# One transformer-like kernel: two v buffers, another pace of the transfers, the last pair's scaling moved into the next stage, and the first pair's scores as products of 64 rows

## The chip, the cores and the metric

The kernel runs on one core of one Trainium2 chip. The metric is the device time of one launch in microseconds (us). Before the change it was 1083.71 us, the median of three runs (1082.7 to 1085.96).

## The reference

Attention over 4 batches of 8 heads (576 tokens, 64 columns a head) that keeps only scores within tau of the row's maximum, then two feed-forward layers over the 2304 tokens:

```
scores = q @ k.T / 8;  thresh = max(scores, row) - tau
scores = where(scores >= thresh, scores, -1e9)
attn = exp(scores - max);  attn = attn / (sum(attn) + 1e-9);  a = attn @ v        # x: 2304 x 512
h = x @ w_in;  g = h * tanh(softplus(h));  x2 = g @ w_out                         # 512 -> 2048 -> 512
y = (silu(x2 @ w_gate) * (x2 @ w_val)) @ w_out2                                   # 512 -> 1536 -> 512
```

## The kernel before, in words

**Pairs.** Attention works through 16 pairs of heads, one after the other, overlapped. The two heads of a pair lie in the upper and the lower 64 partitions of q and k. Each fp32 operand is split into a high part (`qh`, `kh`, rounded to fp32r) and the rest (`ql`, `kl`, L222 to L228); a product of scores is high times high plus the two mixed ones. For pairs 1 to 15 SyncE (SP in the profile) copies these parts into one tile `stk` by 12 transfers a pair (L237), head by head, so that 128 rows hold the high and low parts of one head: then a score tile of 128 queries by 576 keys takes four matmuls (L95: two products, each in columns of 320 and 256). Pair 0 has no such copies: before the change the other head's 64 rows of its query tile are set to zero (L254), the two heads' parts are made one after the other (L261, L263), and a score tile takes six matmuls of 128 rows (L104).

**One score tile** i of 9 (four pairs of tiles, head by turns, and one that holds the last 64 rows of both heads) goes PE scores, DVE row maximum (L112), POOL threshold (L116), ACT exponential (L122), DVE mask and row sum into `pp` (L130), PE transposes (L159, into `tg`), ACT copies into `pt` (L165 to L172), and PE products with v (L182: `av` 0 after the first four score tiles, `av` 1 after all). The row sums' reciprocals go to DRAM and come back spread over the partitions (`r`, `rs`, L200, L205), and POOL multiplies them into the output `acc` in place (L216). Scores have three PSUM buffers, transposes and av two together.

**Order.** Every engine works through its queue in order. The order is written by a list scheduler (`Plan`) from costs, buffers (`SLOTS`: what takes a buffer waits for who gave it back) and a table of ranks (`RANK`, `PERIOD`). Transfers too: one queue, SP's, issues all of them, so a transfer that waits for its buffer holds what is queued behind it. The tile of v had one buffer, and another one for the last pair only (`vslot`).

**The second stage** (`moes`) makes the layers by a scheme of seven products for eight: `ha`, `hb` (L808) and `y` (L934, L936), from pieces `xp` of x and from weights that ACT (L503, L507, L536), DVE (L511, L514, L540) and POOL (L517) convert while the stage runs. It has a plan of its own, so every engine's queue holds all of attention and then all of this stage. Before the change the scaling of the last pair (L205, L216) stands at the end of attention.

Of the kernel before, what the change touches and what calls it, by code (L numbers as in the profile page):

```python
# [16 lines left out]
P = 128  # L17
# [19 lines left out]
def attention(tc, cst, q, k, v, x, beside, parked, S=576):  # L37
# [31 lines left out]

    def mine(nm, h):  # L70
        return slice(64, 640) if nm == "k" and h == 0 else slice(0, 576)

    def vslot(p):
        return "vz" if p == NP - 1 else "vn"

    def load(p, nm):
        src = dict(q=q, k=k, v=v)[nm][p]
        if nm == "v":
            t = pw.tile([P, 10, 64], F32, tag=vslot(p), name=f"vn{p}", bufs=SLOTS["vn"])
        else:  # L80
            t = pn.tile([P, KW], F32, tag="n", name=f"{nm}n{p}", bufs=SLOTS["n"])[:, 0:src.shape[1]]
        nc.sync.dma_start(out=t, in_=src)
        st[p][nm + "n"] = t


    def scores(p, i):
        d = st[p]
        s = ps.tile([P, 1024], F32, tag="s", name=f"s{p}_{i}", bufs=SLOTS["s"])[:, 192:768]
        d["s", i] = s
        c, h = divmod(i, 2)  # L90
        for c0, n in ((0, 320), (320, 256)):
            if p and i < 8:
                q0, k0 = (colB if h else colA) + 128 * c, 576 * h + c0
                for w in (1, 2):
                    nc.tensor.matmul(out=s[:, c0:c0 + n], lhsT=d["stk"][:, 0, q0:q0 + P], rhs=d["stk"][:, w, k0:k0 + n], start=w == 1, stop=w == 2)  # L95
                continue
            for w, (a, b) in enumerate((("h", "h"), ("l", "h"), ("h", "l"))):
                if i < 8:

                    q0, k0 = 576 * h + 128 * c + 64 * h, mine("k", h).start + c0  # L100
                    lhsT, rhs = d["stk"][:, "hl".index(a), q0:q0 + P], d["k" + b][:, k0:k0 + n]
                else:
                    lhsT, rhs = d["qt"][:, "hl".index(a)], d["k" + b][:, 64 + c0:64 + c0 + n]
                nc.tensor.matmul(out=s[:, c0:c0 + n], lhsT=lhsT, rhs=rhs, start=w == 0, stop=w == 2)  # L104
# [97 lines left out]
    def spread(p):  # L202
        t = st[p]["rs"] = pw.tile([P, S], F32, tag="rs", name=f"rs{p}", bufs=SLOTS["rs"])
        for a, c0, n, at in ((0, 0, S, 0), (64, 0, 512, 640), (64, 512, 64, 576)):
            nc.sync.dma_start(out=t[a:a + 64, c0:c0 + n], in_=parked[p][at:at + n].partition_broadcast(64))  # L205

    def xout(p, u):
        for to, c0, c1 in xslices(p, 256 * u, 256 + 64 * u):
            if XOUT[u] == "DVE":
                nc.vector.tensor_copy(out=to, in_=st[p]["av", u][:, c0:c1])  # L210
            else:
                nc.scalar.copy(out=to, in_=st[p]["av", u][:, c0:c1])

# [26 lines left out]
    def tails(p):  # L240
        d = st[p]
        d["qt"] = qt[p % 2]
        for w in range(2):
            for h in range(2):
                a = slice(64 * h, 64 * h + 64)
                t = d["q" + "hl"[w]] if p else d["stk"][:, w, 576 * h:576 * h + 576]
# [3 lines left out]
    def zeros(p):  # L250
        d = st[p]
        d["stk"] = pw.tile([P, 3, 1152], F32R, tag="stk", name=f"stk{p}", bufs=SLOTS["stk"])
        for h in range(2):
            nc.gpsimd.memset(f(d["stk"][64 - 64 * h:128 - 64 * h, 0:2, 576 * h:576 * h + 576]), 0.0)  # L254

    def firstparts(p, what, h):
        d = st[p]
        a, cols = slice(64 * h, 64 * h + 64), slice(576 * h, 576 * h + 576)
        hi, lo = (d["stk"][a, w, cols] for w in range(2))
        if what == "hi":  # L260
            nc.scalar.copy(out=hi, in_=d["qn"][a])  # L261
        else:
            nc.vector.tensor_tensor(out=lo, in0=d["qn"][a], in1=f(hi), op=ALU.subtract)  # L263


    turns = {}
    for tag in "gs":
        line = [(PERIOD * p + r, (p, k, i)) for p in range(NP) for k in "STA" for i, r in enumerate(RANK[k + OWN.get(p, "")]) if (k == "S" or f"{k}{i}" in SIDE) == (tag == "s")]
        turns.update({x: (tag, n) for n, (_, x) in enumerate(sorted(line))})
    plan = Plan(SLOTS, WAIT)  # L270
    for p in range(NP):
# [7 lines left out]
        for nm in "qk":  # L279
            op("DMA", .6, load, nm, key=(nm, "load"), take=["n"])  # L280
            if nm == "q":
                op(*(("Pool", (.72, .74), inputs, "q", "scale", nc.gpsimd) if p else ("DVE", .4, inputs, "q", "scale", nc.vector)), key=("q", "scale"), after=[("q", "load")])
            if nm == "q" and p == 0:
                op("Pool", (2.4, 2.42), zeros, key=("q", "zeros"), take=["stk"])
                for h in range(2):
# [5 lines left out]
        op("Pool", (1.13, 1.15), tails, key=("t",), after=[("q", "stack", 1) if p else ("q", "lo", 1)], take=["qt"], free=["q"] * (p > 0))  # L291
        op("DMA", .6, load, "v", key=("v", "load"), take=[vslot(p)])
        for nm, cost in (("q", 1.2), ("k", 2.4)) * (p > 0):
            for h in range(2):
                op("DMA", cost, stack, nm, h, key=(nm, "stack", h), after=[(nm, "lo"), ("q", "stack", 0)][:2 if (nm, h) != ("q", 0) else 1], take=["stk"] * ((nm, h) == ("q", 0)))
        for i in range(9):
            c, h = divmod(i, 2)
            made = [(y, "stack", z) for y in "qk" for z in ([h] if i < 8 else [0, 1])] if p else [("q", "lo", h if i < 8 else 1), ("k", "lo")]
            op("PE", (.53, .74) if p and i < 8 else (.81, 1.03), scores, i, key=("S", i), after=made + [("t",)] * (i == 8), take=[turns[p, "S", i]], free=["k", "qt", "stk"] if i == 8 else [])
            op("DVE", (.67, .753), rowmax, i, key=("R", i), after=[("S", i)] + [("R", 0)] * (i > 0), take=["sm"] * (i == 0))  # L300
# [7 lines left out]
            if i in (3, 8):  # L308
                u = int(i == 8)
                ready = [("V", y, z) for y in ((0, 1), (2, 3))[u] for z in (0, 3, 6)] + [("V", 4, 0), ("V", 4, 4), ("A", 0)] * u + [("v", "load")]  # L310
                t = 5 * (.432, .538)[u]
                op("PE", (t, t + .22), av, u, 0, 5, key=("A", u), after=ready, take=[turns[p, "A", u]], free=["pt"] + [vslot(p)] * u)
                t = .335 + .07 * u
                op(XOUT[u], (t, t + .09) if XOUT[u] == "DVE" else (.255 + .05 * u, .37 + .05 * u), xout, u, key=("x", u), after=[("A", u)], free=[turns[p, "A", u]])
# [3 lines left out]
        op("DMA", 1.7, park, key=("o", "out"), after=[("Z",)], free=["rr"])  # L318
        op("DMA", 1.3, spread, key=("i", "in"), after=[("o", "out")], take=["rs"])
# [6 lines left out]
    ctx.close()  # L326


class Plan:
# [46 lines left out]
    def order(self, ops, strict):  # L376
# [8 lines left out]
        for o in ops:  # L385
            before = [(made[x], True) for x in o["after"] if x not in self.given]
            for x, k in o["take"]:
                if (x, k - 1) in took:
# [75 lines left out]
GIVEN = dict(DMA=1.0)  # L464
# [4 lines left out]
WARM = 30  # L469
KW = 640  # L470
SLOTS = dict(raw=2, wcu=1, wcl=2, wcn=3, sb=1, wa=2, wb=2, wc=2, xo=1, sm=4, s=3, g=2, e=4, pp=3, pt=2, rr=2, rs=2, q=2, k=2, qt=2, vn=1, vz=1, stk=2, n=2)

PERIOD = 21.7858
# [167 lines left out]
def moes(tc, cp, acc, W, early, where, w_in, w_out, w_gate, w_val, w_out2, out):  # L641
# [329 lines left out]
    ctx.close()  # L971


FETCH = 60
FIRST = -1000
STAGED = (2, 0),
HOLD = 1000000000.0
# [134 lines left out]
```

## Time and profile before

| | |
|---|---|
| median of three runs | 1083.71 us |
| the profiled execution: its time, its span | 1081.55 us, 1079.8 us |
| TensorE busy by the page, share of the span | 1054.3 us, 98% |
| first matmul of the second stage | at 283.66 us |

The page's shares are over the whole span. PE's rows overlap one another, since a matmul's row begins when it starts and ends when its last column is out; so the time of PE is read from its idle gaps ("idle before", with what ended them) and from the granted clock of a stretch, and a share of 98% only tells that few gaps are left. The first 284 us are attention, the rest is the second stage.

### The profile page before, as it was taken

To read this page: it belongs to the slowest core of one execution; us is meant where nothing else is said; L and a number is where in the kernel's file an instruction comes from. 1 tells how busy PE (TensorE), PEld (TensorE's weight loads), DVE (VectorE), ACT (ScalarE), POOL (GpSimd) and SP (SyncE) were. 2 spreads that over 40 slices of the span, in tenths; PEclk is the share of its full clock that TensorE was granted. 3 is DMA by queue.
4 is the path that set the end of the run, shared out by engine and by line. 5 is a ranking of instruction groups with operands and counts; after the bars stand their busy time and mean duration, and the time that the engine had idled before them with its cause. 6 is when DMAs were issued, how large, how long until landed. Compare 5 with 4: busy or idle time off the path is not lost.

```text
span 1079.8 us, 17817 instructions
## 1 busy us (share of the span) xinstructions
PE 1054.3 (98%) x6292; PEld 969.2 (90%) x6292; DVE 776.3 (72%) x1438; ACT 651.2 (60%) x1286; POOL 262.3 (24%) x403
## 2 busy tenths in 40 slices
PE   8899899999899999999999999999999999999998
PEld 7777777777699999999999999999999999999997
DVE  6888888888599565458367766984778686786645
ACT  6788889888688675455356655764454454444331
POOL 4457677764311110022001001010111011010000
PEclk9999999999999999999999999999999999999999
DMA  5767776876877776577567586588888788787793
GB/s 148 204 185 204 205 211 171 241 210 179 286 279 254 272 259 242 175 256 254 181 216 254 189 345 243 237 293 331 300 297 298 256 292 318 268 291 251 238 305 119
DMA packets 71177, 263.46 MB, mean 244 GB/s; under 512 B 11696, under 2 KB 11952, under 8 KB 71088
## 3 DMA queue, kind: packets, MB, share of 16 engines
q1 hardware_dynamic: 71088, 262.32, 72.5%
q8 instruction: 50, 0.82, 0.3%
q14 instruction: 39, 0.32, 0.1%
HBM read 197.92 MB, written 37.82 MB: 218 GB/s over the span
## 4 chain that ended last, share of the span: by engine, by line
PE 87%; DMA 5%; ACT 3%; DVE 2%; issue 1%; SPq 1%; POOL 1%; DVEq 0%; ACTq 0%; POOLq 0%
PE ha L808 22%; PE y L934 18%; PE hb L808 17%; PE y L936 14%; PE av L182 6%; PE tg L159 5%; PE s L95 4%; DMA vn<-in_dram 2%; ACT e L122 1%; PE s L104 1%; ACT pt L165 1%; DMA qn<-in_dram 1%; ACT pt L168 1%; DMA xp<-x10T 1%; DMA rs<-r 1%
## 5 line engine op out<-in xcount | busy, mean ns | idle before, releaser
L517 POOL TENSOR_TENSOR cn<-cn,cl 128x512 int32<-128x512 int32 x68 | 92.5, 1361 | 627.0 <-DVE cn L514 453.9
L934 PE MATMUL y<-g,wo 128*128 128x384 f32 x1152 | 227.6, 334 | 0.7 <-DVE wo L540 0.7
L934 PEld LDWEIGHTS y<-g,wo 128*128 128x128 f32 x1152 | 202.1, 188 | 1.1 <-DVE wo L540 1.0
L952 DVE TENSOR_TENSOR acc<-y,acc 128x512 f32<-128x512 f32 (+2 forms) x163 | 100.0, 625 | 107.9 <-PE y L936 63.3
L936 PE MATMUL y<-wo,g 128*128 128x512 f32 (+1 forms) x654 | 166.6, 391 | 0.0
L808 PE MATMUL hb<-xp,wb 128*128 128x384 f32 x720 | 138.5, 334 | 3.2 <-ACT s L819 3.2
L808 PE MATMUL ha<-xp,wb 128*128 128x384 f32 x720 | 138.3, 334 | 0.0
L936 PEld LDWEIGHTS y<-wo,g 128*128 128x128 f32 x654 | 120.5, 188 | 18.9
L808 PEld LDWEIGHTS hb<-xp,wb 128*128 128x128 f32 x720 | 126.3, 188 | 5.1 <-ACT s L819 3.5
L808 PEld LDWEIGHTS ha<-xp,wb 128*128 128x128 f32 x720 | 126.6, 188 | 3.1
L844 DVE TENSOR_TENSOR g<-c,g 128x384 fp32r<-128x384 f32 x168 | 102.3, 610 | 33.1 <-ACT g L841 32.0
L112 DVE TENSOR_REDUCE sm<-s 128x1 f32<-128x576 f32 x144 | 105.9, 753 | 27.8 <-PE s L95 17.5
L841 ACT CAST g<-c 128x384 fp32r<-128x384 f32 x168 | 86.4, 514 | 63.3 <-DVE c L877 31.0
L130 DVE SCALAR_TENSOR_TENSOR pp<-s,sm,e 128x576 f32<-128x576 f32 x144 | 114.3, 811 | 10.5 <-ACT e L122 6.3
L122 ACT ACTIVATE e<-s,sm 128x576 f32<-128x576 f32 x144 | 105.3, 755 | 5.4 <-DVE sm L112 4.6
L159 PE MATMUL tg<-idf,pp 128*128 128x128 f32 x656 | 104.5, 282 | 2.5 <-ACT pt L168 2.2
L853 ACT ACTIVATE c<-c 128x384 f32<-128x384 f32 x144 | 75.4, 525 | 52.2 <-DVE c L829 51.8
L165 ACT COPY pt<-tg 128x384 f32<-128x384 f32 x192 | 88.2, 487 | 28.6 <-PE tg L159 26.5
L819 ACT COPY u<-ha 128x384 f32<-128x384 f32 x60 | 28.9, 481 | 111.5 <-PE ha L808 111.2
L95 PE MATMUL s<-stk 128*128 128x320 f32 x480 | 93.8, 317 | 1.2 <-DVE sm L112 0.6
L182 PE MATMUL av<-pt,vn 128*64 128x256 f32 (+1 forms) x640 | 85.9, 415 | 9.1 <-DMA vn<-in_dram 6.5
L159 PEld LDWEIGHTS tg<-idf,pp 128*128 128x128 f32 x656 | 72.4, 141 | 24.8 <-issue 7.6
(92 smaller groups left out, 1528.5 us busy)
## 6 DMA issues: line engine op xcount, KB each, us to landing
raw<-in_dram SPq DMA_DIRECT2D x68, 512.0 KB
xp<-x20T SPq DMA_DIRECT2D x24, 768.0 KB
xp<-x21T SPq DMA_DIRECT2D x20, 768.0 KB
xp<-x22T SPq DMA_DIRECT2D x20, 768.0 KB
xp<-x20B SPq DMA_DIRECT2D x18, 768.0 KB
xp<-x10T SPq DMA_DIRECT2D x15, 768.0 KB
xp<-x21B SPq DMA_DIRECT2D x15, 768.0 KB
xp<-x22B SPq DMA_DIRECT2D x15, 768.0 KB
```

What stands on the lines that cost most here:

```text
L95: nc.tensor.matmul(out=s[:, c0:c0 + n], lhsT=d["stk"][:, 0, q0:q0 + P], rhs=d["stk"][:, w, k0:k0 + n], start=w == 1, stop=w == 2)
L112: nc.vector.tensor_reduce(out=d["nm"][:, i:i + 1], in_=d["s", i], op=ALU.max, axis=AX.X, negate=True)
L122: nc.scalar.activation(out=e, in_=d["s", i], func=AF.Exp, bias=d["nm"][:, i:i + 1])
L130: nc.vector.scalar_tensor_tensor(out=d["pp", c][:, 576 * h:576 * h + 576], in0=d["s", i], scalar=d["th"][:, i:i + 1], in1=d["e", i], op0=A ...
L159: nc.tensor.transpose(g[:, 128 * m:128 * m + 128], d["pp", c][:, o:o + 128], idf)
L165: nc.scalar.copy(out=t[:, m0:m0 + n, 128 * (c % 2):128 * (c % 2) + 128], in_=g[:, 0:n])
L182: nc.tensor.matmul(out=d["av", u][64 * h:64 * h + 64, 0:n], lhsT=d["vn"][:, 5 * h + j], rhs=d["pt", u][:, 5 * h + j if j < 4 else 4, 0:n], ...
L808: nc.tensor.matmul(out=tiles[bank, q], lhsT=w[:, a, w0 + P * d:w0 + P * d + P], rhs=x[:, z, d], start=k in (1, 5, 2) and d == 0 and y == 0 ...
L844: (V if GLOW[L] == "DVE" else nc.gpsimd).tensor_tensor(out=tiles["g", j, s][:, 1], in0=tiles[nm, q], in1=f(tiles["g", j, s][:, 0]), op=ALU ...
L934: nc.tensor.matmul(out=y[:, 0:C], lhsT=w[:, a, P * d:P * d + P], rhs=h[:, x], **m)
L936: nc.tensor.matmul(out=y[:, c0:c1], lhsT=h[:, x, P * d:P * d + P], rhs=w[:, a, c0:c1], **m)
L952: V.tensor_tensor(out=a, in0=y, in1=a, op=ALU.add)
```

## The change

Five parts. (1) v has two buffers for all pairs (`vn=2`), so the v of a pair may be loaded while the pair before it still uses its own. (2) The plan has other costs for transfers, and a new table of ranks. (3) The last pair's `rs` transfers and its scaling are no longer in attention's plan but in that of the second stage, in a tile of that stage (`sb`), held until its times 4 and 12. (4) Its av is copied out by ACT, not DVE. (5) Pair 0 has no zeros and no separate parts for each head; its scores are products of 64 rows, head 0 from partitions 0 to 63 and head 1 from 64 to 127, the matmuls of the two heads by turns, with both tiles' PSUM buffers taken at once (`SPLIT`).

```diff
-    def vslot(p):
-        return "vz" if p == NP - 1 else "vn"
...
+        both = range(2) if split(p) and i < 8 else range(1)
+        for h in both:
+            d["s", i + h] = ps.tile([P, 1024], F32, tag="s", name=f"s{p}_{i + h}", bufs=SLOTS["s"])[:, 192:768]
...
             for w, (a, b) in enumerate((("h", "h"), ("l", "h"), ("h", "l"))):
-                if i < 8:
-
-                    q0, k0 = 576 * h + 128 * c + 64 * h, mine("k", h).start + c0
-                    lhsT, rhs = d["stk"][:, "hl".index(a), q0:q0 + P], d["k" + b][:, k0:k0 + n]
...
+                for h in both:
+                    if i < 8:
+                        rows, q0, k0 = slice(64 * h, 64 * h + 64), 128 * c + 64 * h, mine("k", h).start + c0
+                        lhsT, rhs = d["q" + a][rows, q0:q0 + P], d["k" + b][rows, k0:k0 + n]
...
-            if nm == "q" and p == 0:
-                op("Pool", (2.4, 2.42), zeros, key=("q", "zeros"), take=["stk"])
-                for h in range(2):
-                    op("ACT", (.573, .671), firstparts, "hi", h, key=("q", "hi", h), after=[("q", "scale"), ("q", "zeros")])
-                    op("DVE", (.66, .755), firstparts, "lo", h, key=("q", "lo", h), after=[("q", "hi", h)], free=["n"] * h)
-                continue
...
-        op("DMA", .6, load, "v", key=("v", "load"), take=[vslot(p)])
+        op("DMA", 1.0, load, "v", key=("v", "load"), take=["vn"])
...
-        op("DMA", 1.7, park, key=("o", "out"), after=[("Z",)], free=["rr"])
-        op("DMA", 1.3, spread, key=("i", "in"), after=[("o", "out")], take=["rs"])
+        op("DMA", 1.4, park, key=("o", "out"), after=[("Z",)], free=["rr"])
+        if p == NP - 1:
+            break
+        op("DMA", 1.9, spread, key=("i", "in"), after=[("o", "out")], take=["rs"])
         op("Pool", (1.42, 1.45), scaled, key=("n",), after=[("x", 0), ("x", 1), ("i", "in")], free=["rs"])
...
-GIVEN = dict(DMA=1.0)
+GIVEN = dict(DMA=2.0)
...
-PERIOD = 21.7858
+PERIOD = 31.9948
...
+    last = plan.new("sb")
+    plan.op("DMA", 1.9, lambda: late[0](pm.tile([P, 1024], F32, tag="sb", name="sb", bufs=MSLOTS["sb"])[:, 0:576]), ("last", "in"), [], [last], [], LAST[0])
+    plan.ops[-1]["hold"] = LAST[0]
+    plan.op("Pool", 1.45, late[1], ("last", "n"), [("last", "in")], [], [last], LAST[1])
...
+LAST = 4.0, 12.0
```

The table of ranks sets the order on every engine. Three places show what it does. The names in the rows carry the pair's number (`vn5` is v of pair 5; `s0_2` is score tile 2 of pair 0).

SP's queue around the load of v of pair 5, before:

```order
L237 DMA stk6_1398<-qh6_1337 64x576
L237 DMA stk6_1398<-ql6_1337 64x576
L499 DMA raw_1592<-in_4_dram 128x1024
L82 DMA qn8_1611<-in_0_dram 128x576
L82 DMA vn5_1617<-in_2_dram 128x640
L200 DMA r4_120<-rr0_155 9x32 x4
L237 DMA stk7_1661<-qh7_1565 64x576
L237 DMA stk7_1661<-ql7_1584 64x576
```

and after:

```order
L202 DMA r3_119<-rr1_156 9x32 x4
L82 DMA kn6_1345<-in_1_dram 128x640
L628 DMA x10B11_74<-xo_1147 128x1536
L242 DMA stk6_1393<-qh6_1348 64x576
L242 DMA stk6_1393<-ql6_1366 64x576
L207 DMA rs3_1424<-r3_119 64x576
L207 DMA rs3_1424<-r3_119 64x512
L207 DMA rs3_1424<-r3_119 64x64
L82 DMA qn7_1444<-in_0_dram 128x576
L82 DMA vn5_1461<-in_2_dram 128x640
L242 DMA stk6_1393<-qh6_1348 64x576
L242 DMA stk6_1393<-ql6_1366 64x576
```

The load of v has moved ahead by most of a pair: from behind all copies for pair 6 to ahead of ten of the twelve. The loads of q and v now stand ahead of the copies of k, and the load of k directly behind `r`.

TensorE's queue at the start of pair 0, before:

```order
L104 MATMUL s0_0_212<-kh0_205,stk0_194 128x320 x2
L104 MATMUL s0_0_212<-kl0_210,stk0_194 128x320
L104 MATMUL s0_0_212<-kh0_205,stk0_194 128x256 x2
L104 MATMUL s0_0_212<-kl0_210,stk0_194 128x256
L104 MATMUL s0_1_221<-kh0_205,stk0_194 128x320 x2
L104 MATMUL s0_1_221<-kl0_210,stk0_194 128x320
L104 MATMUL s0_1_221<-kh0_205,stk0_194 128x256 x2
L104 MATMUL s0_1_221<-kl0_210,stk0_194 128x256
```

and after, from the last products of tiles 0 and 1 to the first transposes:

```order
L106 MATMUL s0_0_211<-kl0_207,qh0_201 128x256
L106 MATMUL s0_1_212<-kl0_207,qh0_201 128x256
L106 MATMUL s0_2_244<-kh0_203,qh0_201 128x320
L106 MATMUL s0_3_245<-kh0_203,qh0_201 128x320
L106 MATMUL s0_2_244<-kh0_203,ql0_205 128x320
L106 MATMUL s0_3_245<-kh0_203,ql0_205 128x320
```

Two tiles are now made together, by turns of the two heads, twelve matmuls for both.

POOL's queue where attention ends, before (`sm` is a threshold or sum, `rs15` the spread reciprocals of the last pair):

```order
L216 TENSOR_TENSOR acc_63<-acc_63,rs14_4071 128x576
L186 TENSOR_SCALAR sm15_3894<-sm15_3894 128x9
L216 TENSOR_TENSOR acc_63<-acc_63,rs15_4170 128x576
L517 TENSOR_TENSOR cn_4217<-cn_4217,cl_4228 128x512
L517 TENSOR_TENSOR cn_4226<-cn_4226,cl_4256 128x512
```

and after:

```order
L221 TENSOR_TENSOR acc<-acc,rs_4030 128x576
L118 TENSOR_SCALAR sm_3891<-sm_3891,tau 128x1 x2
L188 TENSOR_SCALAR sm_3891<-sm_3891 128x9
L511 TENSOR_TENSOR cn<-cn,cl 128x512 x2
L221 TENSOR_TENSOR acc<-acc,sb 128x576
L511 TENSOR_TENSOR cn<-cn,cl 128x512 x62
```

The last pair's scaling stands behind the first two weight conversions, not ahead of them. On the other engines the order of the second stage is that of before from about a dozen entries on.

## Rows read from the trace of the kernel before

**Rows 1.** Windows: stretch, length, each engine's busy us (rows), granted clock, DMA share, GB/s

```profile
240.00:260.00 20.00, 19.77 (x153) 15.55 (x150) 17.19 (x38) 16.47 (x36) 12.88 (x25) 1.00 0.75 206
...
320.00:340.00 20.00, 20.00 (x117) 20.00 (x117) 19.08 (x32) 17.60 (x35) 3.36 (x3) 1.00 0.69 248
```

**Rows 2.** Waits of PE, start to 460 us: total, times, longest

```profile
PE av L182 <- DMA vn<-in_dram: 6.5, 5, 2.6
PE hb L808 <- ACT s L819: 3.2, 1, 3.2
...
PE y L934 <- DVE wo L540: 0.7, 1, 0.7
```

**Rows 3.** Timeline, pairs 1 and 5: start, us, engine, line, [idle before <- releaser]

```profile
38.47 0.39 SPq L82 DMA_DIRECT2D vn<-in_dram  x1
...
43.22 2.38 PE L182 MATMUL av<-pt,vn 128*64 128x256 f32 x20 [2.08 <-DMA vn<-in_dram]
...
46.75 1.62 DVE L112 TENSOR_REDUCE sm<-s 128x1 f32<-128x576 f32 x2 [2.61 <-PE s L95]
...
112.50 3.65 PE L182 MATMUL av<-pt,vn 128*64 128x256 f32 x20 [2.61 <-DMA vn<-in_dram]
```

**Rows 4.** Chain of waits, 100 to 130 us: start, us, what

```profile
106.45 5.91 DMA vn<-in_dram
```

**Rows 5.** Windows around the long wait of pair 5, and in pair 0

```profile
109.90:113.40 3.50, 0.91 (x9) 0.76 (x11) 3.29 (x7) 2.83 (x5) 2.45 (x4) 1.00 0.73 176
113.40:116.85 3.45, 3.45 (x18) 2.15 (x15) 0.72 (x2) 0.43 (x2) 1.32 (x2) 0.51 0.72 258
...
14.45:17.85 3.40, 3.40 (x17) 3.32 (x16) 2.47 (x6) 2.24 (x4) 2.04 (x3) 0.50 0.82 254
```

**Rows 6.** Timeline, first product with v of pairs 13 and 14 (windows of 2 us)

```profile
244.88 1.30 PE L182 MATMUL av<-pt,vn 128*64 128x256 f32 x10
...
260.93 1.30 PE L182 MATMUL av<-pt,vn 128*64 128x256 f32 x10
```

**Rows 7.** Timeline of pair 0

```profile
5.64 1.37 ACT L261 CAST stk<-qn 64x576 fp32r<-64x576 f32 x2 [3.63 <-DVE qn L222]
6.34 1.54 DVE L263 TENSOR_TENSOR stk<-qn,stk 64x576 fp32r<-64x576 f32 x2 [0.74 <-ACT stk L261]
...
11.80 0.82 DVE L130 SCALAR_TENSOR_TENSOR pp<-s,sm,e 128x576 f32<-128x576 f32 x1 [0.78 <-POOL sm L116]
```

**Rows 8.** Chain of waits in pair 0: a score tile at half and at full clock

```profile
14.17 1.53 PE s L104 x6
...
18.57 0.79 PE s L104 x6
```

**Rows 9.** Groups by shape, 0 to 284 us: busy, mean ns of one, idle before

```profile
L95 PE MATMUL s<-stk 128*128 128x256 f32 x240 | 47.9, 281 | 0.0
...
L182 PE MATMUL av<-pt,vn 128*64 128x256 f32 x320 | 39.3, 392 | 8.7 <-DMA vn<-in_dram 6.5 <-ACT kh L225 1.1 <-ACT pt L165 1.0
...
L95 PEld LDWEIGHTS s<-stk 128*128 128x128 f32 x480 | 71.4, 190 | 4.5 <-DVE pp L130 2.0 <-DVE sm L112 0.8
L182 PEld LDWEIGHTS av<-pt,vn 128*64 128x64 f32 x640 | 46.3, 138 | 37.3 <-ACT pt L165 3.8 <-issue 3.0 <-ACT e L122 2.3
```

**Rows 10.** Timeline where attention ends and the second stage begins

```profile
288.68 1.40 POOL L216 TENSOR_TENSOR acc<-acc,rs 128x576 f32<-128x576 f32 x1 [7.77 <-DMA rs<-r]
...
291.33 0.62 ACT L536 CAST wo<-cn 128x512 fp32r<-128x512 f32 x1 [3.74 <-POOL cn L517]
...
292.38 1.31 PE L808 MATMUL hb<-xp,wb 128*128 128x384 f32 x6 [3.22 <-ACT s L819]
```

**Rows 11.** Waits of SP's queue, 0 to 300 us

```profile
SPq L82 <- POOL kl L228: 27.3, 11, 3.8
```

**Rows 12.** Timeline: last copy for pair 11 and its second score tile

```profile
190.55 0.60 SPq L237 DMA_DIRECT2D stk<-ql  x1
...
194.72 0.78 PE L95 MATMUL s<-stk 128*128 128x320 f32 x4
```

More of the change, by code (lines that the diff above doesn't have):

```diff
@@ L200, in park, with spread @@
             nc.sync.dma_start(out=to[:, b], in_=rr[p % 2][32 * b:32 * b + 9, 1])
-    def spread(p):
-        t = st[p]["rs"] = pw.tile([P, S], F32, tag="rs", name=f"rs{p}", bufs=SLOTS["rs"])
+    def spread(p, into=None):
+        t = st[p]["rs"] = into if into is not None else pw.tile([P, S], F32, tag="rs", name=f"rs{p}", bufs=SLOTS["rs"])
         for a, c0, n, at in ((0, 0, S, 0), (64, 0, 512, 640), (64, 512, 64, 576)):
@@ L212, in xout, with gone @@
                 nc.scalar.copy(out=to, in_=st[p]["av", u][:, c0:c1])
+    def gone(p, u):
+        return "ACT" if p == NP - 1 else XOUT[u]
     def scaled(p):
@@ L245, in tails, with ranked @@
                 a = slice(64 * h, 64 * h + 64)
-                t = d["q" + "hl"[w]] if p else d["stk"][:, w, 576 * h:576 * h + 576]
+                t = d["q" + "hl"[w]]
                 nc.gpsimd.tensor_scalar(out=d["qt"][a, w, a], in0=f(t[a, 512 - 512 * h:576 - 512 * h]), scalar1=1.0, scalar2=1.0, op0=ALU.mult, op1=ALU.mult)
-    def zeros(p):
-        d = st[p]
-        d["stk"] = pw.tile([P, 3, 1152], F32R, tag="stk", name=f"stk{p}", bufs=SLOTS["stk"])
-        for h in range(2):
[L254 to L263, printed above, removed]
+    def ranked(p, k):
+        r = RANK[k + OWN.get(p, "")]
+        return [r[i // 2] + .001 * (i % 2) for i in range(9)] if k == "S" and split(p) else r
     turns = {}
     for tag in "gs":
-        line = [(PERIOD * p + r, (p, k, i)) for p in range(NP) for k in "STA" for i, r in enumerate(RANK[k + OWN.get(p, "")]) if (k == "S" or f"{k}{i}" in SIDE) == (tag == "s")]
+        line = [(PERIOD * p + r, (p, k, i)) for p in range(NP) for k in "STA" for i, r in enumerate(ranked(p, k)) if (k == "S" or f"{k}{i}" in SIDE) == (tag == "s")]
         turns.update({x: (tag, n) for n, (_, x) in enumerate(sorted(line))})
@@ L297, in attention @@
             c, h = divmod(i, 2)
-            made = [(y, "stack", z) for y in "qk" for z in ([h] if i < 8 else [0, 1])] if p else [("q", "lo", h if i < 8 else 1), ("k", "lo")]
-            op("PE", (.53, .74) if p and i < 8 else (.81, 1.03), scores, i, key=("S", i), after=made + [("t",)] * (i == 8), take=[turns[p, "S", i]], free=["k", "qt", "stk"] if i == 8 else [])
-            op("DVE", (.67, .753), rowmax, i, key=("R", i), after=[("S", i)] + [("R", 0)] * (i > 0), take=["sm"] * (i == 0))
+            made = [("q", "lo"), ("k", "lo")] if split(p) else [(y, "stack", z) for y in "qk" for z in ([h] if i < 8 else [0, 1])]
+            if not (split(p) and h):
+                n = 2 if split(p) and i < 8 else 1
+                t = .77 if n == 2 else .53 if i < 8 else .81
+                op("PE", (t, t + .21), scores, i, key=("S", i), after=made + [("t",)] * (i == 8) + [("S", 6)] * (i == 8), take=[turns[p, "S", i + z] for z in range(n)], free=["k", "qt"] + ["q" if split(p) else "stk"] if i == 8 else [])
+            op("DVE", (.67, .753), rowmax, i, key=("R", i), after=[("S", i - i % 2 if split(p) else i)] + [("R", 0)] * (i > 0), take=["sm"] * (i == 0))
             op("Pool", (.225, .264), thresh, i, key=("H", i), after=[("R", i)])
@@ L311, in attention @@
                 t = 5 * (.432, .538)[u]
-                op("PE", (t, t + .22), av, u, 0, 5, key=("A", u), after=ready, take=[turns[p, "A", u]], free=["pt"] + [vslot(p)] * u)
+                op("PE", (t, t + .22), av, u, 0, 5, key=("A", u), after=ready, take=[turns[p, "A", u]], free=["pt"] + ["vn"] * u)
                 t = .335 + .07 * u
-                op(XOUT[u], (t, t + .09) if XOUT[u] == "DVE" else (.255 + .05 * u, .37 + .05 * u), xout, u, key=("x", u), after=[("A", u)], free=[turns[p, "A", u]])
+                op(gone(p, u), (t, t + .09) if gone(p, u) == "DVE" else (.255 + .05 * u, .37 + .05 * u), xout, u, key=("x", u), after=[("A", u)], free=[turns[p, "A", u]])
         op("Pool", (.225, .253), added, key=("P",), after=[("M", 7), ("M", 8)])
@@ L326, in attention @@
     ctx.close()
+    return lambda into: spread(NP - 1, into), lambda: scaled(NP - 1)
 class Plan:
@@ L387, in order @@
             for x, k in o["take"]:
-                if (x, k - 1) in took:
+                if (x, k - 1) in took and took[x, k - 1] is not o:
                     before.append((took[x, k - 1], False))
@@ L1037, in beside @@
             first.store(plan, nm, room, XEARLY + n, ["xo"])
-    attention(tc, cst, q, k, v, x, beside, parked)
-    moes(tc, cp, acc, W, early, where, w_in, w_out, w_gate, w_val, w_out2, out)
+    late = attention(tc, cst, q, k, v, x, beside, parked)
+    moes(tc, cp, acc, W, early, where, late, w_in, w_out, w_gate, w_val, w_out2, out)
 CHUNK = 384
```

36 lines of the change are left out of this document (19 added, 17 removed).

## The prediction

> **What bounds the kernel now.** I read the windows first, to see which engine has no time left in each part. In the second stage PE has no gap in 20 us at full clock; in a quiet stretch of attention it still lacks only 0.23 us of 20, while DVE and ACT each have some 3 us free [rows 1]. So PE bounds both, and what can be gained is PE's gaps, its half clock, and PE work itself. The waits of PE come next: before 460 us the largest are 6.5 us in five waits for the load of v, one of 3.2 us for an ACT copy, and 0.7 us for a weight of the second stage [rows 2]. Third, the timeline at these waits. The load of v of pair 1 is issued at 38.47 us and its product starts at 43.22, after 2.08 us of idle PE; DVE then stands idle for 2.61 us because PE sends it nothing, so the wait is not hidden by another engine [rows 3]. In pair 5 the load took 5.91 us to land [rows 4] and PE waited 2.61 [rows 3]; right behind that wait PE's granted clock is 0.51 for 3.45 us, which is the level of 1.2 GHz for nearly all of the stretch [rows 5], and the product took 3.65 us instead of 2.38 [rows 3]. Fourth, the pace: the first products with v of pairs 13 and 14 start 260.93 - 244.88 = 16.05 us apart [rows 6], but from pair 1 (43.22) to pair 14 (260.93) it is 217.7 us for 13 pairs, 16.75 each [rows 3, 6]. PE's 13 pairs thus hold 217.7 - 13 x 16.05 = 9.0 us more than at the pace of a quiet one.
>
> **The change part by part.** The sum is made against the profiled execution, 1081.55 us (span 1079.8).
>
> *Two v buffers.* Before, a load of v could go only when the product with v of the pair before had ended. Now it waits for the pair before that, and its place in SP's queue is earlier by most of a pair. That is about 16 us of lead [rows 6] against a longest landing of 5.91 [rows 4]. So all five waits go: -6.5 us [rows 2]. What is late next is the transposed tile: 1.0 and 1.1 us of waits for ACT stand ahead of the same products already [rows 9], and I leave them. If the cover fails the term is nothing. Bounds 0 and -6.5.
>
> *The half clock after the wait of pair 5.* 3.45 us at 0.51 [rows 5] hold what full clock does in 1.75, so -1.7 if PE no longer idles there. The stretch before it had PE busy for 0.91 of 3.50 us [rows 5]; without the wait it has 2.6 us more. Bounds -1.7 and, if another such stretch appears elsewhere, +1.7; I take -1.7.
>
> *The new order and costs.* Of the 9.0 us of excess, at most 4.4 are waits for v (6.5 less the 2.1 of pair 1, which lie before the stretch), and 1.7 is the clock. That leaves 2.9 us for other reasons. The new ranks may close or widen them. Bounds -2.9 and, if the two waits for ACT doubled, +2.1; I take -0.8, nearer to no change, since neither the work of ACT nor that of DVE gets less.
>
> *The last pair's scaling.* POOL stood idle for 7.77 us for the spread reciprocals, scaled until 290.08, and only then came to the weight conversion; ACT waited 3.74 us for that with a cast, PE's bank was copied out behind the cast, and PE waited 3.22 [rows 10]. Now two conversions stand ahead of the scaling, so the cast no longer waits for the reciprocals. ACT's 3.74 us are more than PE's 3.22, so the wait goes whole: -3.2. The scaling itself then lies in POOL's idle time, of which the second stage has 16.6 us in 20 [rows 1]. Bounds 0 and -3.9 (with the 0.7 us for `wo` [rows 2]). The last av on ACT instead of DVE: nothing, both were idle there.
>
> *Pair 0.* The zeros go at no gain: the cast that writes beside them waited for DVE's scaled q, not for POOL [rows 7]. One cast and one subtraction over 128 partitions take the place of two each over 64; the two subtractions were 1.54 us [rows 7], so the first row maximum comes 0.75 us earlier. The first mask stood 0.78 us for POOL's threshold [rows 7], behind the scaling of q of pair 1; the new queue has the first threshold ahead of it, so up to -0.78 more. Then two tiles are made at once. A tile took 0.79 us at full clock [rows 8]. Does a pair of 64-row matmuls take as long as one of 128 rows, or as two? No row shows 64 rows, but the product with v uses 64 of the 128 columns by turns of the heads: a row of it lasts 392 ns against 281 for the same 256 columns of a score [rows 9], and yet 20 of them fit in 2.38 us [rows 3], 119 ns apart. So each streams for about twice as long and two run side by side. By that nearest row a group for two tiles costs 0.79; if nothing runs side by side, 1.58. Between lie the weight loads: 190 ns for 128 columns and 138 for 64 [rows 9], so 104 ns grow with 128 columns, and 12 loads one after another are 1.25 us. I take 0.79. Three of the four groups lie in the chain (a group needs two of three PSUM buffers and so a mask first), and the upper bound adds 3 x 0.79 = 2.4 us. The clock: in pair 0 a stretch of 3.40 us had half clock [rows 5], a tile then took 1.53 [rows 8]. The new pair 0 has less PE work between its waits, so I let two more groups run slow: +1.5. Of these 1.5 I take 1.0: -0.75 - 0.78 + 1.0 = -0.5. Bounds: one slow tile fewer than before, -0.75 - 0.78 - 0.74 = -2.3, and all against it, -1.53 + 1.5 + 2.4 = +2.4.
>
> The Trainium skill ("TensorE: Matmul & The Clock Gate", on LDWEIGHTS) has the time of a weight load go by columns and not by rows, which speaks against halving the rows: by its 128 / 1.2 GHz = 107 ns (an estimate from that page) a group is 12 loads, 1.28 us, and the whole comes out 1.5 us later. By that rule, the step of 52 ns for 64 columns agrees [rows 9]; no row shows whether loads of two halves run side by side.
>
> The skill's page "TensorEngine Tiling (Array Packing)", Key Properties, says that a change of the tiling drains the engine. Pair 0 now changes six times between 64-row groups and transposes. No row prices it; a drain can be no longer than a matmul's own row, 281 ns [rows 9], so by that rule the whole is at most 1.7 us later.
>
> *Sum.* -6.5 - 1.7 - 0.8 - 3.2 - 0.5 = -12.7, so 1068.9 for an execution like the profiled one. The median of the runs lies 2.2 above that execution; I add half, since part of what differs from run to run should be the waits that go. Forecast **1070**, its own range 1066 to 1074.
>
> **The rivals.**
>
> *All pairs at 16.05.* The new order closes the 2.9 us too, pair 0 gains its 2.3 and the `wo` wait goes: -6.5 - 1.7 - 2.9 - 3.9 - 2.3 = -17.3, with 1.1 for the median 1065.4. For it: PE is the only full engine in a quiet stretch [rows 1]. Against: DVE and ACT have 3 us of 20 left, and less in the pairs that also convert weights.
>
> *The v wait covered another.* If the masks or ACT's copies are just behind v, attention keeps its time and only the handover and pair 0 gain: 1081.55 - 3.7 = 1077.9, with 1.1 for the median 1079. For it: DVE is busy 17.19 of 20 [rows 1]. Against: DVE's idle 2.61 at that very wait [rows 3].
>
> *The halves don't run side by side* (the change doesn't do what it says): +2.4, and with the drains 1073.
>
> *The copies for the scores come late* (slower). The loads of q and v now stand ahead of the eight copies of k. Before, the last copy of pair 11 was issued at 190.55 and its second tile started at 194.72 without a wait [rows 12], a lead of 4.2 us; two loads of about 0.5 us issue ahead make it 3.2. A transfer that lands in 4.6 us, as v did behind a full queue (issued at 38.47, used at 43.22 [rows 3]), is then 1.4 late in each of 14 pairs: +19.6 - 12.7 = +6.9, with 1.1 for the median 1089.5. It decides from a landing of 4.1 (0.9 us a pair). For it: the transfer engines are busy 75% of the time in the quiet stretch [rows 1]. Against: SP stood for 27.3 us in 11 waits until k's buffer was free [rows 11], 2.5 us a pair at a place that is now ahead of the copies; the load of k moved up, so copies should go earlier, not later.
>
> **How the numbers follow.** Forecast 0.58, all pairs at 16.05 0.12, halves not side by side 0.10, v covered another 0.13, copies late 0.07. A difference of 0.3% (3.25 us) is about what a measurement of this kernel can tell from none, so faster is below 1080.5 and slower above 1087. The first three cases are faster, and half of the fourth (1079 lies close to the line): 0.80 + 0.06 = 0.86. The rest of the fourth is the same, 0.07, and late copies are slower, 0.07. The range 1063 to 1079 leaves out the late copies and the outer halves of two rivals.
>
> **What would show it.** Right: no wait of PE for v in any pair; the first products with v about 16.2 us apart throughout; granted clock 1.0 from some 25 us on; the first matmul of the second stage near 274; no wait of `hb` for ACT behind it; POOL's idle for the late reciprocals without a waiter. The row maxima of tiles 2 and 3 near 12 us mean that the halves run side by side; 13 and later that they don't. Wrong: PE waits for `stk`, or new waits of the same size for ACT or DVE ahead of the products with v; a pace of 16.7 in spite of v on time; half clock over most of pair 0.

## The result

The changed kernel takes 1073.75 us (median of 4 runs, 1072.5 to 1074.38) against 1083.43 of the kernel before on the same chip (4 runs, 1082.7 to 1085.96): ratio 0.9905, 95% interval 0.9886 to 0.9924, so 9.7 us less. The forecast was 1070 with a range of 1063 to 1079: the direction and the range held, the time lies 3.75 above the forecast. The profiled execution took 1074.05 us (span 1072.2), 7.5 less than the profiled one before.

The waits of PE after, from the start to 460 us (total, times, longest), to be laid beside [rows 2]:

```profile
PE s L106 <- DVE pp L132: 4.1, 2, 2.5
PE tg L158 <- ACT pt L170: 2.2, 2, 1.1
...
PE y L933 <- DVE wo L534: 0.8, 1, 0.8
...
PE y L933 <- ACT wo L530: 0.8, 1, 0.8
```

The same view of the kernel before has for the first two:

```profile
PE tg L159 <- ACT pt L168: 2.2, 12, 0.2
PE s L104 <- DVE pp L130: 1.8, 1, 1.8
```

No wait for v is left, and none of `hb` for ACT. The waits of scores for a mask in pair 0 grew from one of 1.8 us to two of together 4.1, as the timeline will show. Waits of transposes for ACT's copies were there before too, 2.2 us in twelve short ones; now two of 1.1 us stand out, one in pair 5 and one in pair 6.

Windows after (stretch, length, busy us of PE, PEld, DVE, ACT, POOL with their rows, granted clock, DMA share, GB/s). The first stands for the quiet stretch of [rows 1], the next two for the wait of pair 5, the last for pair 0 [rows 5]:

```profile
240.00:260.00 20.00, 19.89 (x156) 15.31 (x155) 17.53 (x41) 16.44 (x36) 10.35 (x26) 1.00 0.66 185
...
106.45:110.00 3.55, 3.55 (x32) 2.75 (x32) 3.08 (x7) 3.29 (x8) 1.03 (x4) 1.00 0.71 202
110.00:113.40 3.40, 3.40 (x29) 3.04 (x25) 3.40 (x9) 1.98 (x7) 1.64 (x3) 1.00 0.91 266
16.65:23.45 6.80, 6.50 (x31) 5.36 (x30) 3.86 (x9) 4.47 (x9) 1.75 (x5) 0.50 0.86 222
```

The half clock behind pair 5 is gone and PE has no gap in these two stretches (one of its waits of 1.1 us follows at 113.6). But in pair 0 the stretch at 0.50, which is 1.2 GHz, is now 6.80 us long; before it was 3.40. This is the profiled execution, with a mean granted clock of 0.996; one of the four runs had 1.000 and took 1072.5.

The timeline of PE in pair 0 (start, us, engine, line, tile, [idle before <- releaser]) shows what stood ahead of it:

```profile
8.46 0.30 PE L106 MATMUL s<-kh,qh 64*128 64x320 f32 x1
11.27 0.38 PE L106 MATMUL s<-kh,qh 64*128 64x320 f32 x1 [2.51 <-DVE pp L132]
11.28 0.52 PE L106 MATMUL s<-kh,ql 64*128 64x320 f32 x2
...
11.91 0.39 PE L106 MATMUL s<-kl,qh 64*128 64x256 f32 x2
12.23 0.88 PE L161 MATMUL tg<-idf,pp 128*128 128x128 f32 x6
13.04 0.41 PE L106 MATMUL s<-kh,qh 64*128 64x320 f32 x1
15.01 0.38 PE L106 MATMUL s<-kh,qh 64*128 64x320 f32 x1 [1.57 <-DVE pp L132]
```

Three buffers hold scores and a group fills two. The third buffer lets one head start at 8.46, and since the heads go by turns PE then stands until the mask of the first tile has freed another: 2.51 us, and again 1.57. Before, three tiles were made ahead and PE stood once.

On DVE the row maxima of pair 0 (two in a row) and its first mask answer to [rows 7]:

```profile
8.66 1.42 DVE L114 TENSOR_REDUCE sm<-s 128x1 f32<-128x576 f32 x2 [0.86 <-PE s L106]
10.30 0.82 DVE L132 SCALAR_TENSOR_TENSOR pp<-s,sm,e 128x576 f32<-128x576 f32 x1 [0.22 <-ACT e L124]
...
12.23 1.42 DVE L114 TENSOR_REDUCE sm<-s 128x1 f32<-128x576 f32 x2 [0.37 <-PE s L106]
...
15.97 1.42 DVE L114 TENSOR_REDUCE sm<-s 128x1 f32<-128x576 f32 x2
```

The first mask came at 10.30 instead of 11.80, the 1.5 us that the forecast gave it. The second group's maxima start at 12.23, where the forecast had its sign that the halves run side by side. That sign alone doesn't tell, since the run with one head after the other has them at 11.85; what does tell stands with that run and in the rows of the weight loads below. From there a group takes 3.74 us (12.23 to 15.97).

The first products with v of pairs 1 and 14, against [rows 3, 6]:

```profile
42.44 0.87 PE L184 MATMUL av<-pt,vn 128*64 128x256 f32 x6
...
256.11 1.08 PE L184 MATMUL av<-pt,vn 128*64 128x256 f32 x8
```

From pair 1 to pair 14 it is now 213.67 us, 16.44 a pair, where it was 217.71.

Where the second stage begins (all engines), against [rows 10]:

```profile
279.02 2.35 PE L807 MATMUL ha<-xp,wa 128*128 128x384 f32 x12 [0.52 <-ACT acc L214]
...
281.21 4.32 PE L807 MATMUL hb<-xp,wb 128*128 128x384 f32 x24
...
282.82 0.62 ACT L530 CAST wo<-cn 128x512 fp32r<-128x512 f32 x1
...
285.37 4.33 PE L807 MATMUL ha<-xp,wb 128*128 128x384 f32 x24
...
289.41 1.43 POOL L221 TENSOR_TENSOR acc<-acc,sb 128x576 f32<-128x576 f32 x1 [3.95 <-DMA sb<-r]
```

POOL still waits for the last reciprocals (3.95 us), but behind two conversions; the cast of `wo` and `hb` stand for nothing.

### The profile page after: what moved, and what is told of

The parts are those of the page before. It is cut to its first block, busy times and chain, and to the rows that moved or that the text cites. A ratio compares the mean times of both kernels' runs of the same rounds, so it can differ in the third digit from the quotient of the medians.

```text
span 1072.2 us, 17806 instructions
## 1 busy us (share of the span) xinstructions
PE 1054.5 (98%) x6292; PEld 964.9 (90%) x6292; DVE 773.1 (72%) x1436; ACT 650.1 (61%) x1286; POOL 262.4 (24%) x401
## 4 chain that ended last, share of the span: by engine, by line
PE 86%; DVE 5%; POOL 4%; ACT 2%; issue 2%; DMA 0%; SPq 0%; DVEq 0%; POOLq 0%; ACTq 0%
PE ha L807 23%; PE y L933 18%; PE hb L807 17%; PE y L935 14%; PE av L184 5%; PE tg L161 4%; PE s L97 3%; DVE sm L114 2%; DVE pp L132 2%; ACT e L124 1%; PE s L106 1%; POOL sm L118 1%; PE warm L68 1%; ACT pt L167 1%; POOL qn L227 0%
## 5 line engine op out<-in xcount | busy, mean ns | idle before, releaser
L161 PE MATMUL tg<-idf,pp 128*128 128x128 f32 x656 | 102.1, 283 | 2.4 <-ACT pt L167 1.0
```

The costliest lines, as they stand in the source:

```text
L161: nc.tensor.transpose(g[:, 128 * m:128 * m + 128], d["pp", c][:, o:o + 128], idf)
```

## The experiments

All ratios are to the kernel before, run on the same chip; 0.001 is 1.1 us. Different chips gave that kernel 1083.1 to 1084.5, so runs are compared by ratio.

**Two v buffers alone.**

```diff
-        return "vz" if p == NP - 1 else "vn"
+        return "vn"
-SLOTS = dict(..., vn=1, vz=1, ...)
+SLOTS = dict(..., vn=2, ...)
```

> The kernel before with one edit: two v buffers for all pairs; its table of ranks, its costs and everything else stay. Theory A (the gain of attention is the waits for v, and the buffers alone take them away): no wait of PE for v, no half clock behind pair 5, 6 to 8 us less than before, about 1076. Theory B (the loads go early only because the new ranks move them up SP's queue; behind the old queue they stay late): waits for v of 3 us or more remain and the time is within 2.5 us of before, 1081 to 1084.

Measured 1084.51, ratio 1.0011 (0.9997 to 1.0025). Waits of PE, start to 460 us:

```profile
PE av L182 <- DMA vn<-in_dram: 5.2, 5, 2.5
PE hb L808 <- ACT s L819: 3.5, 1, 3.5
```

Theory A fell: the buffer alone is worth nothing. SP's queue tells why; it is one row after another, so no buffer lets a load overtake:

```profile
36.80 1.33 SPq L237 DMA_DIRECT2D stk<-ql  x1
38.23 0.53 SPq L82 DMA_DIRECT2D qn<-in_dram  x1
38.80 0.46 SPq L82 DMA_DIRECT2D vn<-in_dram  x1
```

The load of v of pair 1 went at 38.80, before at 38.47 [rows 3]: behind copies and the load of q of pair 4, free buffer or not.

**The late scaling alone.**

```diff
+        if p == NP - 1:
+            break
         op("DMA", 1.3, spread, key=("i", "in"), ...)
...
+    plan.op("DMA", 1.9, lambda: late[0](...), ("last", "in"), ..., LAST[0])
+    plan.op("Pool", 1.45, late[1], ("last", "n"), ..., LAST[1])
...
-xz=(123.03, 260.43,)
+xz=(123.03, 295.43,)
```

> The kernel before with one edit: the last pair's spread and scaling are issued by the second stage behind two weight conversions, as in the changed kernel (and its av copies both go to ACT). Theory A (the 3.2 us that PE waited for hb go whole): about 1080, and no wait of hb for ACT. Theory B (the wait only moves, to the pieces that need the scaled columns or to a weight cast behind them): 0 to 1 us less, 1082.5 to 1083.5, with a new wait of 2 us or more in the first 30 us of the second stage.

(The last copy of av now stands in ACT's queue, behind the copies that it needs: `xz`.) Measured 1078.65, ratio 0.996 (0.9945 to 0.9976), -4.3 us, and the wait of `hb` is 0.2 us in place of 3.2. Theory A holds.

**The groups of the first pair alone** (the changed kernel's `scores`, `tails` and plan for pair 0; old ranks, one for each group).

```diff
-        s = ps.tile([P, 1024], F32, tag="s", ...)[:, 192:768]
+        both = range(2) if split(p) and i < 8 else range(1)
+        for h in both:
+            d["s", i + h] = ps.tile([P, 1024], F32, tag="s", ...)[:, 192:768]
...
-S0=(-152.82, -125.34, -81.68, -64.18, -60.83, -57.35, -47.74, -38.02, -32.37,)
+S0=(-152.82, -81.68, -60.83, -47.74, -32.37,)
```

> The kernel before with one edit: the first pair's scores as groups of two tiles, products of 64 rows, heads by turns; its ranks stay, one for each group. Theory A (from the trace of the changed kernel: groups in lockstep for two PSUM buffers leave PE idle and bring the half clock, pair 0 ends 1.9 us later): about 1085. Theory B (as forecast, the shorter preparation outweighs it): about 1083. Row maxima of the third and fourth tile 3.5 us behind the first two in either case.

Measured 1085.96, ratio 1.0029 (1.0016 to 1.0041): 3.1 us slower. A window of pair 0:

```profile
11.00:24.65 13.65, 11.08 (x54) 8.41 (x54) 8.20 (x17) 6.72 (x13) 5.41 (x13) 0.50 0.67 170
```

13.65 us at half clock, where [rows 5] has 3.40. It begins inside an idle stretch of PE of 3.27 us, which ends at 12.02.

**All three edits, old ranks and costs** (the three diffs above together).

> The kernel before with all three edits (two v buffers, late scaling, groups in the first pair), but with its own ranks and costs. Against the changed kernel it differs by ranks, costs and the planner's limits alone. Theory A (the edits bring the gain, the numbers next to nothing): 1073 to 1075, as the changed kernel (1073.75). Theory B (the new numbers are needed to use the buffers): 1078 or more. If the old order were better: below 1072.

Measured 1081.35, ratio 0.9981 (0.9968 to 0.9994). Theory B: most of the gain isn't there without the new numbers. PE waits 3.2 us for v, and pair 0 has 10.24 us of half clock. Which of the new numbers is it?

**Two v buffers, and v's loads one pair earlier in SP's queue** (three ranks lowered by the old period; from pair 2 on the loads then stand behind the same load of q as in the changed kernel).

```diff
-Dv1=(55.06,), ... Dvz=(56.51,), ... Dv=(51.68,)
+Dv1=(33.27,), ... Dvz=(34.72,), ... Dv=(29.89,)
```

> The kernel before with two v buffers and, in its table of ranks, the rank of v's load lowered by one pair (21.79 us), so that each load of v stands one pair earlier in SP's queue; all other ranks stay. Theory C (the wait needs both: a free buffer and an earlier place in SP's queue, since with the buffers alone 5.2 us of waits stayed): no wait for v, 5 to 8 us less than before in the median, 1075 to 1078, and the runs lie closer together (before 1080 to 1087). Theory D (what is behind v, masks and ACT's copies, takes its place): 1081 to 1084.

Measured 1079.04, ratio 0.9964 (0.995 to 0.9977), -3.9 us. No wait for v is left, theory C, though the sum is below its 5 to 8. In the profile the second stage starts 6.5 us earlier (277.19, before 283.66), but what stands behind takes part of it back. Waits of PE, and the timeline of POOL there:

```profile
PE hb L808 <- ACT s L819: 6.0, 1, 6.0
```

```profile
284.95 1.40 POOL L216 TENSOR_TENSOR acc<-acc,rs 128x576 f32<-128x576 f32 x1 [8.31 <-DMA rs<-r]
```

PE's wait behind the last reciprocals grew from 3.2 [rows 2] to 6.0, and 6.83 us of half clock began in it, at 286.5. The runs didn't come closer together either (1076.84 to 1084.66).

**The same with the late scaling** (this diff, the first and the second together).

> As the run before it (two v buffers, v's loads one pair earlier), and the late scaling of the last pair; the first pair stays as in the kernel before, with full-row products. Theory C: the two gains add, 1083.1 less 6 less 4.5, about 1072.5, at or below the changed kernel (1073.75), because the groups of the first pair cost 2.8 us when made alone. Theory D: about 1078, as the late scaling alone; then the rest of the changed kernel's gain is in its other ranks.

Measured 1073.74, ratio 0.9916 (0.9903 to 0.9929), -9.1 us. This is the changed kernel's time, within its interval, without the groups of the first pair and with all other ranks old.

**That, with the groups of the first pair** (all three edits, v's loads early).

> The kernel before with all three edits and v's loads one pair earlier in SP's queue; its other ranks and costs stay. It differs from the run with buffers, earlier loads and late scaling (1073.74) by the groups of the first pair alone, and from the changed kernel (1073.75) by the other ranks and costs alone. Theory C (the groups cost 2 to 3 us under the old ranks, and the other new ranks give that back): 1075.5 to 1077. Theory G (with v on time the groups cost nothing): 1073 to 1074.5, and then the other ranks are worth nothing either.

Measured 1076.75, ratio 0.9936 (0.9915 to 0.9958), 2.2 us above the run without the groups by the ratios, 3.4 above the changed kernel. This leans to theory C (the groups cost again, and the rest of the new numbers gives about that back), but the interval overlaps those of both kernels, so the sizes are rough. The profiles agree on the groups: the first product with v of pair 0 starts at 25.61 here, at 22.98 without the groups and at 23.75 in the changed kernel. Of the 1.9 us by which this kernel is behind the changed one there, only 0.4 is left at the second stage (279.45, after 279.02). The clock of the runs goes with their times: its mean is 0.991 or 0.992 in four of six here (1076.42 to 1077.61), 0.996 in the two fastest (1074.86 and 1074.99); the changed kernel's four had 0.996 to 1.000.

**The changed kernel with v's loads one pair later.**

```diff
-Dv1=(-122.15,), ... Dvz=(25.89,), ... Dv=(32.77,)
+Dv1=(64.76,), ... Dvz=(57.88,), ... Dv=(64.76,)
```

> The changed kernel with one edit: the rank of v's load raised by one pair, so that each load (from the second pair's on) stands again behind the load of q of the third pair after it, as in the kernel before; two buffers stay. Theory C (the place in SP's queue, not the buffer, sets when v is there): waits for v of 3 to 8 us come back and the median is 3 to 7 us above the changed kernel, 1077 to 1081. Rival (the buffer is enough with the new order of everything else): 1073 to 1075.

Measured 1167.95, ratio 1.078 (1.0755 to 1.0805): the mechanism of theory C, at more than ten times its price. Waits of PE, and the chain of waits (start, us, what) from the product of pair 4 towards that of pair 5:

```profile
PE av L184 <- DMA vn<-in_dram: 67.6, 12, 6.4
```

```profile
114.28 4.01 PE av L184 x20
...
126.64 0.54 POOL sm L118 x2
127.17 0.73 POOL qn L227
...
127.93 0.68 ACT qh L230
...
128.68 1.44 POOL ql L233
...
130.14 0.47 SPq L242
...
133.21 5.22 DMA vn<-in_dram
```

The trace shows a ring. SP issues the load of v behind a copy of `ql`; POOL makes `ql` behind its thresholds, these follow row maxima that come late because the product with v was late. The load was issued at 133.21 and the next product started at 138.56, 24.3 us after the one of pair 4; so each round takes 24 us in place of 16. Part of that is the clock: the product of pair 4 took 4.01 us, not 2.38, and the mean granted clock of this execution is 0.959.

**One head after the other in a group.**

```diff
-        for c0, n in ((0, 320), (320, 256)):
+        for one, c0, n in [(h, c0, n) for h in both for c0, n in ((0, 320), (320, 256))]:
...
-                for h in both:
+                for h in (one,):
```

> The changed kernel with the twelve 64-row matmuls of a group in another order: the six of one head, then the six of the other; the same products, waits and places. If the halves run side by side only by turns (a group takes about 0.8 us by turns), a group now takes 1.4 us or more, its second row maximum is no earlier and pair 0 ends 0.5 to 2 us later: 1074.5 to 1076. If the turns don't matter: a group stays below 0.95 us and the time is 1073 to 1074.5.

Measured 1074.94, ratio 0.9929 (0.9917 to 0.9942): 1.2 us above the changed kernel by the medians, 2.6 by the ratios, whose intervals overlap. The second head's six of the second group:

```profile
11.34 0.38 PE L106 MATMUL s<-kh,qh 64*128 64x320 f32 x1 [1.83 <-DVE pp L132]
11.56 0.31 PE L106 MATMUL s<-kh,ql 64*128 64x320 f32 x1
11.71 0.31 PE L106 MATMUL s<-kl,qh 64*128 64x320 f32 x1
11.86 0.28 PE L106 MATMUL s<-kh,qh 64*128 64x256 f32 x1
11.97 0.28 PE L106 MATMUL s<-kh,ql 64*128 64x256 f32 x1
12.09 0.28 PE L106 MATMUL s<-kl,qh 64*128 64x256 f32 x1
12.30 0.87 PE L161 MATMUL tg<-idf,pp 128*128 128x128 f32 x6
```

Six of one head take 1.03 us (11.34 to 12.37); in the changed kernel eleven of both heads take 1.03 as well (11.27 to 12.30). So the halves run side by side by turns. Yet the gain is small: in this order the first head's six run ahead, in time in which PE would stand idle (1.83 us of idle here, 2.51 there). My expectation of the price (up to 2 us) fits, its reason only in part.

**Extra matmuls in the idle stretches of pair 0.**

```diff
+        if p == 0 and i in FILL:
+            w = bank(f"fill{i}")
+            for _ in range(FILL[i]):
+                nc.tensor.matmul(out=w[:, 0:256], lhsT=d["qh"][:, 0:P], rhs=d["kh"][:, 0:256], start=True, stop=True)
...
+FILL = {2: 20, 4: 12}
```

> The changed kernel with 20 matmuls of 128x256 into an unused bank ahead of the second group of the first pair and 12 ahead of the third, in the 2.5 and 1.6 us in which PE stood idle. Theory E (the half clock over 6.8 us of pair 0 follows from these idle stretches): granted clock 1.0 or one short stretch in pair 0, 1 to 3 us less than the changed kernel, about 1072. Theory F (half clock comes anyway, or pair 0 waits for DVE and ACT and not for PE): 1073.5 or more, up to 1 us worse where the extra matmuls stand in the way.

Measured 1072.98, ratio 0.991 (0.9897 to 0.9923), no different from the changed kernel's. The windows show both halves of the answer:

```profile
16.65:23.45 6.80, 5.87 (x50) 4.44 (x50) 5.96 (x12) 5.73 (x12) 2.09 (x7) 1.00 0.88 237
298.45:301.90 3.45, 3.45 (x13) 3.45 (x12) 3.45 (x4) 0.34 (x2) 1.83 (x1) 0.51 0.63 256
```

Theory E was right on the cause: with PE kept busy the clock of pair 0 stays at 1.00 and the second stage starts 2.0 us earlier (277.07, after 279.02). But then a stretch at 0.51 came at 298.5, behind the two waits for `wo`, and the span is 1071.9, hardly less than without the extra work (1072.2). The changed kernel's profile has the same two waits, 0.76 and 0.85 us, and full clock behind them; so the waits alone don't bring the half clock, and why it came in this execution is open.

**Extra matmuls there as well.** The 28 write columns of a bank in which other sums are still open, so neither this run nor the next one computes the reference; only their time counts.

```diff
+                            if idle == j and d == 0 and z < 2:
+                                for _ in range(14):
+                                    nc.tensor.matmul(out=y[:, C:512], lhsT=h[:, 0, 0:P], rhs=h[:, 0, 0:512 - C], ...)
```

> The changed kernel with the extra matmuls in the first pair (median 1072.98) and 28 more of 128x128 in front of two products of the second stage, where PE waited 0.76 and 0.86 us for a weight; they write columns that nothing reads. Theory E (the half clock that some runs show near 298 us follows from these idle stretches): granted clock 1.0 from the first pair to the end in every run, 1071 to 1072.3. Theory F (it comes anyway, or the extra work delays the products): 1072.5 to 1074.

Measured 1074.15, ratio 0.9911 (0.9892 to 0.9929); the granted clock is 1.0 in five of six runs and 0.999 in one. Theory E on the clock, theory F on the time. The timeline:

```profile
296.21 1.67 PE L938 MATMUL y<-g 128*128 128x128 f32 x14
297.72 0.39 PE L941 MATMUL y<-g,wo 128*128 128x384 f32 x1
297.95 1.67 PE L938 MATMUL y<-g 128*128 128x128 f32 x14
299.46 1.10 PE L941 MATMUL y<-g,wo 128*128 128x384 f32 x5
```

I sized them wrongly: 14 take 1.51 us (296.21 to 297.72) where PE had stood 0.76 and 0.86. They cost 3.0 us and hide 1.6, so 1.4 of the 1.7 that the clock gives was spent again. Half as many were not tried.

**The two v edits, the late scaling and both fillings, without groups.**

> The kernel before with two v buffers, v's loads one pair earlier, the late scaling (median 1073.74, fastest run 1071.56 at granted clock 1.000), and extra matmuls in the 1.9 us idle stretch of the first pair and in front of the two late products of the second stage. Theory E: clock 1.0 in every run, 1070.5 to 1072, ahead of the changed kernel. Theory F (the clock is not what spreads the runs): 1073 to 1074.5.

Measured 1075.77, ratio 0.9925 (0.9905 to 0.9945), clock 0.998 to 1.000. Theory F: the run with the best parts was no better, and its four runs with a mean clock of 1.000 still reach from 1074.37 to 1076.33, so the clock is not what spreads them. Its profiled execution and that of the same kernel without fillings both had full clock, and yet the spans are 1074.5 and 1069.8; 3.9 of these 4.7 us stand already at the first matmul of the second stage (279.86 and 275.99). So they are lost in attention; by what is open. No kernel here is measurably ahead of the changed one.

## Why the prediction held, and where it was off

First the whole, profile against profile: the second stage was to start 9.5 us earlier (6.5 + 1.7 + 0.8 + 0.5) and started 4.6 earlier (279.02, in the trace of before 283.66); behind that point 3.2 were to go and 3.0 went (7.6 of the span, less 4.6). So the handover was sized well and attention was not.

*Two v buffers.* The waits went, all 6.5 us. The step gave as reasons the free buffer and the earlier place in SP's queue together: the buffer alone brought 1.0011 and 5.2 us of waits, both 0.9964 and none, and the changed kernel with the old place 1.078. So the place is needed beside the buffer; whether the early place would do with one buffer was not run. That the waits come back whole as time was too much to expect (see the new order).

*The half clock behind pair 5.* Gone, as forecast (0.51 [rows 5], now 1.00). But it was not a sure price of the wait: with two buffers alone PE waited 2.47 us ahead of the same product (at 111.65), and it took 2.38 us, at full clock.

*The last pair's scaling.* -3.2 forecast, -4.3 (-6.0 to -2.6) alone. What the step lacked is that it protects the v gain: without it the wait of `hb` grew to 6.0.

*Pair 0.* This is the step that failed. I took -0.5 with bounds of -2.3 and +2.4. The 1.5 us at the first mask came, and a group runs side by side for about the price of one tile, as the row of the product with v had it. The working even says that a group needs two of three buffers and so a mask first, but it puts no price on that: PE stands 2.51 and 1.57 us, where it stood once for 1.75. The half clock behind that lasts 6.80 us instead of 3.40. So pair 0's own first product with v is 0.57 late (23.75, before 23.18) instead of 0.5 early. The one of pair 1 came 0.78 us earlier (42.44, before 43.22 [rows 3]); with that pair's wait of 2.08 gone and -0.5 it should have been 2.6. So up to there +1.3 stands in place of -0.5; the 0.7 that came between the two products is not shown to be the groups'. Under the old ranks the groups alone cost 3.1 us, and roughly 2.2 with v on time. The rival "the halves don't run side by side" came near the measured time by luck: its 1073 lies between 1072.4 (1070 + 2.4) and 1074.1 (with all of the 1.7 for drains), and its reason was wrong.

That the halves run side by side is seen in the weight loads of pair 0 too (PEld, after): two of them, one of each head, are done in 0.19 us, and a single one takes 0.18.

```profile
8.11 0.19 PEld L106 LDWEIGHTS s<-kh,ql 64*128 64x128 f32 x2
...
11.24 0.18 PEld L106 LDWEIGHTS s<-kh,qh 64*128 64x128 f32 x1 [2.71 <-issue]
```

By the Trainium skill's rule on weight loads ("TensorE: Matmul & The Clock Gate", LDWEIGHTS) the twelve loads of a group would have taken 1.28 us and eleven of them 1.18, estimates from its 107 ns. The trace doesn't agree: eleven matmuls with their loads took 1.03, as six of one head did, so the loads of the two halves don't add up here.

For a change of tiling the rows show a small price in one direction: with one head after the other the transposes start 0.21 us after the last product of 64 rows (12.09 to 12.30), and before they started 0.12 after one of 128 rows of the same width (13.53 to 13.65). That is 0.09 more, and six times that is 0.5, an estimate, where the forecast's most was 1.7. The drain that the Trainium skill's page "TensorEngine Tiling (Array Packing)", Key Properties, ties to such a change has no row of its own, and no row shows the way back alone.

*The new order.* Forecast -0.8 over pairs 1 to 14. Measured there: 213.67 against 217.71, -4.0 where 4.4 + 1.7 + 0.8 = 6.9 were expected, so 2.9 short. The kernel with the old ranks, v's loads early and the late scaling splits this: it needs 213.0 for the same pairs (40.7 to 253.7). So the waits for v and the half clock gave back 4.7 of 6.1, since others came in part in their place (in that kernel PE waits 1.3 us for a mask and 1.7 for a copy of ACT ahead of the products of pairs 2 and 3); that much of the rival "the v wait covered another" came true. And the new ranks cost 0.7 there instead of bringing 0.8. What they are worth lies in pair 0, if anywhere, where by the profiles they limit the damage of the groups. The rival of late copies did not come: PE waits nowhere for `stk`.

*The median.* I added 1.1, half of the 2.2 by which the median lay above the profiled execution. It lies 0.3 below it now, and the kernel before ran between 1080.32 and 1086.75 in 26 runs. So both gains are true, 7.5 from profile to profile and 9.7 between the medians: one profile of the kernel before stands near the short end of its spread, and the changed kernel's four runs lie within 1.9 us.

From profile to profile the miss is 12.7 - 7.5 = 5.2: the stretch up to the product of pair 1 holds 1.8 of it (1.3 in place of -0.5), the pairs behind it 2.9. The median took 1.4 back (1.1 added, 0.3 below), which leaves the 3.75. That these two misses went against each other is luck.

## What to carry to other kernels

A second buffer is worth nothing while its load stands in an in-order queue behind work that comes late: move the load too, and look at the issue time in the trace to see whether the load really moved. Price a wait that you take away together with the next one at the same place: the v gain reached the end only when the last pair's scaling was moved too. And when two results are made at once, count buffers: two from three leaves one to work ahead, which stops the engine that feeds them.

## What the runs showed that I had not expected

- A load that comes one pair too late can close a ring through SP, PE, DVE, POOL and ACT: 67.6 us of waits where the kernel before, with its load of v behind the same load of q, had 6.5.
- With PE kept busy in pair 0 the 6.8 us at 0.50 were gone, but in the profiled execution a stretch of 3.45 at 0.51 came at 298.5. With both places filled the clock was 1.0 throughout and the time was the same.
- 14 matmuls of 128x128, each with its own weight load, go 108 ns apart (1.51 us for 14). That is hardly less than two 256-column ones of 64 rows by turns take together (11.67, 11.79, 11.91 in the changed kernel, 120 ns for two).
